# A long convolution and a mixture of experts in one kernel: hand-ordered joins between its outer and middle stages, and a middle that works on pairs of groups

## The chip, the cores and the metric

The kernel runs on one core of a Trainium2 chip. The metric is the device time of one execution in microseconds. Three executions were timed before the change; one more was recorded by the hardware profiler, and its trace is what the profile's rows come from.

## What is computed

The first half is a long convolution with a gate, the second a routed expert layer on its rows:

```python
def _attn_ref(x, v, pos_emb, w1, w2):            # x, v: (4, 11456, 128)
    h_filt = (np.maximum(pos_emb @ w1, 0.0) @ w2) * np.exp(-0.01 * pos)[:, None]
    Uf = np.fft.rfft(x * v, n=2 * S, axis=1)
    Hf = np.fft.rfft(h_filt, n=2 * S, axis=0)
    return x * np.fft.irfft(Uf * Hf[None], n=2 * S, axis=1)[:, :S, :]

def _moe_ref(x, modality_id, w_gate, modality_bias, w1, w2):   # x: (45824, 128), 8 experts
    logits = x @ w_gate + modality_bias[modality_id]
    e_idx = np.argmax(logits, axis=1)
    gate_w = softmax(logits)[np.arange(N), e_idx]
    for e in range(E):
        h = np.maximum(x[e_idx == e] @ w1[e], 0.0)             # 128 -> 1024
        out[e_idx == e] = gate_w[e_idx == e, None] * (h @ w2[e])
```

## The kernel before

**Stages.** A transform of length 90 x 64 stands in for the FFT. The filter is transformed first (`filter_stages`, `filter_middle`; its spectra go to `hs` in HBM). Then the four batches alternate between two kinds of stage. An *outer* stage b does three things in 16 steps q at once: the forward transform of batch b (`forward_stages`: load u and v, multiply, transform, copy to `A`), the inverse transform of batch b-1 (`inverse_stages`), and the routing of batch b-1's rows (`route_stages`), which works on 8 output blocks o of two q each. A *middle* stage (`middle_stages`) multiplies the spectra of batch b in 23 groups g of four of the 90 frequencies. Where an outer stage runs into the middle stage of its batch is called a join here; joins 1, 2 and 3 are those of batches 1, 2 and 3. After the last outer stage the expert tiles run (`experts`) to the end.

**A group of the middle stage.** `load(g)` asks on SyncE's queue for the constants b (256 KB) and the filter spectra h (512 KB), `load_c(g)` for the constants c (256 KB). `spectrum(g)` is 16 matmuls on TensorE (L598, 128 rows by 64 columns) into a pair of PSUM banks, pz, of which there are two. Then come its products on VectorE: two multiplications for `more` (L610), two for `part` (L617), one sum (L621). GpSimd does two sums of `more` (L612, L613) and one of `part` (L622). `inverse(g)` is 48 matmuls (L641, 64 rows by 128 columns) and two copies on ScalarE (L645). b, h and c lie in rings of three slots inside the tile `rings`; the outer stage keeps its transposed spectra `w_t` and the transposed rows `xT_t` in the same tile, so a slot can be asked for only when the outer stage no longer reads that place.

**What sets the order.** Every engine but GpSimd runs in the order in which the program calls it, and SyncE's queue of DMA requests too: a request that waits holds up all behind it. `steps` gives each stage function a step from a table (`OUTER`, `MID`: "name:delay"), `overlapped` lays the last steps of one stage beside the first of the next. In a join before the change the last three outer steps lie beside steps 1 to 3 of the middle stage. In a group's step the order is load_c, spectrum (with its products), the inverse of two groups back, load.

**Rows to their experts.** `store` writes an output block to `xr` (two DMAs of 366 KB), `places` writes the row numbers to `xi`. `fetch(b)` reads them back, `rows_back` brings 5 x 128 rows at a time into one of three buffers (18 requests per batch), and `send_rows` issues scatters of 128 rows from GpSimd (L270), 90 per batch, spread over the following middle and outer stage, at most 8 under way.

```python
MID = "load_c:2 spectrum:2 inverse:4 load:0"
OV, EA, EM = 3, 3, 5
```
```python
if b > 0:
    seq = seq[:-EM] + mid[:1] + seq[-EM:]
seq = overlapped(seq, mid[1:] if b else mid, OV if b else F3, b > 0)
```

## Time and profile before

| | us |
|---|---|
| median of three executions | 2121.38 |
| lowest, highest | 2119.81, 2122.85 |
| profiled execution, its own time | 2118.69 |
| its span, first to last instruction | 2116.9 |
| TensorE busy | 2049.2 |
| VectorE busy | 1709.5 |
| ScalarE busy | 1192.2 |
| GpSimd busy | 1195.1 |

The span is what the rows' times count in; the profiled execution took 1.8 us more than its span. A matmul's end is modelled, so the distance between two starts tells more than a duration. PE is TensorE, PEld its weight loads, DVE is VectorE, ACT ScalarE, POOL GpSimd, SPq SyncE's queue of DMA requests. A name after an arrow in brackets is what ended the idle time before a row.

### The profile page before, as it was taken

The page shows a single profiled execution, that of the slowest core. Times are in us where ns is not written, and L with a number is a line of the kernel's source. Part 1 is how long each engine was busy: PE and PEld are TensorE (multiplying, and loading weights), DVE is VectorE, ACT ScalarE, POOL GpSimd, SP SyncE. Part 2 cuts the span into 40 slices and gives each one's busy share as a digit, 9 for nine tenths or more (in the row PEclk, how much of TensorE's full clock was granted, in tenths as well). Part 3 has the DMA queues.
Part 4 walks back from the last instruction along what each step waited for, and adds up shares of the span by engine and source line. Part 5 has one row for each costly group of instructions (what it writes and reads, how often), then busy time and mean ns, then how long its engine had stood idle before and what let it go on. Part 6 is the DMA issues. An engine that isn't in the chain of part 4 may idle for free. (4 is left out here: it accounts for less than half of the span.)

```text
span 2116.9 us, 50221 instructions
## 1 busy us (share of the span) xinstructions
PE 2049.2 (97%) x18162; PEld 1668.1 (79%) x18162; DVE 1709.5 (81%) x2804; ACT 1192.2 (56%) x2166; POOL 1195.1 (56%) x1221
## 2 busy tenths in 40 slices
PE   8989999899999999899999999999999999999996
PEld 8888777687767877687668888888888888888896
DVE  2349767895779957896997888898898998888885
ACT  3642266324761267324666666666666666666674
POOL 0206500497547955497545677777777465555563
PEclk9999999999999999999999999999999999999998
DMA  9577677687879879885688466556565555555310
GB/s 314 214 294 235 234 231 244 217 265 262 302 257 291 263 259 325 271 265 191 207 245 280 83 132 127 124 122 133 125 129 116 111 109 95 100 97 97 79 42 26
DMA packets 509590, 397.55 MB, mean 188 GB/s; under 512 B 372697, under 2 KB 406317, under 8 KB 509337
## 3 DMA queue, kind: packets, MB, share of 16 engines
q1 hardware_dynamic: 482681, 334.90, 56.6%
q0 software_dynamic: 26496, 59.36, 7.9%
q8 instruction: 145, 2.38, 0.5%
q14 instruction: 108, 0.88, 0.1%
q10 hardware_dynamic: 160, 0.03, 0.0%
HBM read 290.58 MB, written 103.96 MB: 186 GB/s over the span
## 5 line engine op out<-in xcount | busy, mean ns | idle before, releaser
L1137 DVE SCALAR_TENSOR_TENSOR hl<-ph,hh 128x512 fp32r<-128x512 f32 x724 | 485.5, 678 | 105.2 <-ACT hh L1136 98.4
L1136 ACT ACTIVATE hh<-ph 128x512 fp32r<-128x512 f32 x724 | 425.2, 598 | 217.4 <-PE ph L1133 211.2
L270 POOL DMA_INDIRECT xs<-back,to x360 | 370.6, 1029 | 226.2 <-DVE y L677 72.6
L1186 POOL DMA_INDIRECT out<-ot,idx x362 | 400.2, 1106 | 144.1 <-issue 114.7
L1133 PE MATMUL ph<-xl,wh 128*128 128x512 f32 (+1 forms) x792 | 296.3, 374 | 4.5 <-DVE xl L1118 4.4
L1131 PE MATMUL ph<-xh,wh 128*128 128x512 f32 (+1 forms) x792 | 298.8, 377 | 0.7 <-ACT xh L1117 0.7
L1132 PE MATMUL ph<-xh,wl 128*128 128x512 f32 (+1 forms) x792 | 294.4, 372 | 1.1 <-DVE wl L1086 1.1
L1154 PE MATMUL po<-hh,wh 128*128 128x512 f32 (+1 forms) x792 | 294.3, 372 | 0.0
L1156 PE MATMUL po<-hl,wh 128*128 128x512 f32 (+1 forms) x792 | 293.8, 371 | 0.0
L1155 PE MATMUL po<-hh,wl 128*128 128x512 f32 (+1 forms) x792 | 293.7, 371 | 0.0
L645 ACT COPY A<-pw 128x512 f32<-128x512 f32 (+1 forms) x184 | 97.1, 579 | 345.1 <-PE pw L641 345.1
L617 DVE TENSOR_TENSOR part<-pz,rings 128x1024 f32<-128x1024 f32 (+1 forms) x184 | 211.3, 1189 | 2.2 <-POOL part L622 2.2
L612 POOL TENSOR_TENSOR more<-more 128x256 f32<-128x256 f32 (+1 forms) x92 | 76.8, 835 | 228.8 <-DVE more L610 217.4
L641 PEld LDWEIGHTS pw<-rings,part 64*128 64x128 f32 x2880 | 175.5, 188 | 35.4 <-issue 28.5
L641 PE MATMUL pw<-rings,part 64*128 64x128 f32 x2880 | 200.2, 278 | 2.5 <-POOL part L622 2.5
L598 PE MATMUL pz<-A,rings 128*64 128x256 f32 x1440 | 177.1, 388 | 13.7 <-DMA rings<-in_c_b 10.8
L466 PE MATMUL s<-fwd,seq 128*64 128x90 f32 x4096 | 170.7, 242 | 5.4 <-issue 4.0
L1133 PEld LDWEIGHTS ph<-xl,wh 128*128 128x128 f32 x792 | 149.3, 189 | 33.1 <-DVE xl L1118 5.8
L466 PEld LDWEIGHTS s<-fwd,seq 128*64 128x64 f32 x4096 | 161.3, 137 | 12.7 <-issue 4.7
L1132 PEld LDWEIGHTS ph<-xh,wl 128*128 128x128 f32 x792 | 149.6, 189 | 26.8 <-DVE wl L1086 1.6
L1131 PEld LDWEIGHTS ph<-xh,wh 128*128 128x128 f32 x792 | 149.4, 189 | 25.9 <-ACT xh L1117 0.9
L1154 PEld LDWEIGHTS po<-hh,wh 128*128 128x128 f32 x792 | 149.1, 188 | 26.1 <-issue 0.7
(190 smaller groups left out, 3662.4 us busy)
## 6 DMA issues: line engine op xcount, KB each, us to landing
rings<-hs SPq DMA_DIRECT2D x88, 512.0 KB
seq<-in_u SPq DMA_DIRECT2D x64, 512.0 KB
seq<-in_v SPq DMA_DIRECT2D x64, 512.0 KB
seq<-in_x SPq DMA_DIRECT2D x64, 512.0 KB
xr<-xo SPq DMA_DIRECT2D x64, 365.6 KB
back<-xr SPq DMA_DIRECT2D x72, 325.0 KB
rings<-in_c_b SPq DMA_DIRECT2D x88, 256.0 KB
rings<-in_c_c SPq DMA_DIRECT2D x88, 256.0 KB
```

The lines of the kernel that those rows point to most:

```text
L270: s = pool.indirect_dma_start(out=xs, out_offset=bass.IndirectOffsetOnAxis(ap=ix, axis=0), in_=src, in_offset=None, bounds_check=E * R - 1 ...
L466: pe.matmul(v[64 * c:64 * c + 64, blk, j], u[:, blk, 4 * h + j], fwd[:, c], start=True, stop=True)
L641: pe.matmul(pw[par][:, to:to + D], t[at], k["c"][at, q, c], start=i == 0, stop=i == len(terms) - 1)
L1131: pe.matmul(p, k[0, "h"][:, f:f + D], k["xh"], start=True, stop=False)
L1132: pe.matmul(p, k[0, "l"][:, f:f + D], k["xh"], start=False, stop=False)
L1133: pe.matmul(p, k[0, "h"][:, f:f + D], k["xl"], start=False, stop=True)
L1136: act.activation(hh, ph, AF.Relu)
L1137: dve.scalar_tensor_tensor(hl, ph, 0.0, hh.bitcast(F32), op0=ALU.max, op1=ALU.subtract)
L1154: pe.matmul(po, k[1, "h"][:, f], hh[:, t], start=g == 0, stop=False)
L1155: pe.matmul(po, k[1, "l"][:, f], hh[:, t], start=False, stop=False)
L1156: pe.matmul(po, k[1, "h"][:, f], hl[:, t], start=False, stop=g == NCH - 1)
L1186: s = pool.indirect_dma_start(out=out, out_offset=bass.IndirectOffsetOnAxis(ap=k["idx"][:, j:j + 1], axis=0), in_=ot[:, j, :], in_offset=N ...
```

## The change

It does six things. The joins of batches 1 to 3 are written out by hand, call by call, in `joined`: the routing of the last output block is taken out of the outer table and placed among the first groups, and the loads for groups 1 to 5 stand at chosen places, most of them ahead of the store of the last block. The ring places of h and b are changed, so that b of groups 1 and 2 no longer lies where `xT_t` lies and h of group 2 does. `spectrum` is split into the matmuls and `products`. From then on the middle stage works by twos: two spectra, their products, then two inverses of the pair before. In batches 1 to 3 the sum that VectorE did (L621) is GpSimd's for groups 0 to 4. The scatters of a middle stage run over groups 6 to 20 instead of 5 to 22, the others move into later stages, and all but the first of a batch's requests for rows are issued by ScalarE instead of SyncE. The second of the last inverse's two copies goes to VectorE, and there are 12 work buffers in place of 11.

```diff
-NA, NXO = 11, 3
+NA, NXO = 12, 3
...
-    def rows_back(b, k):
+    def rows_back(b, k, queue):
...
-        rows_back(b, 0)
+        rows_back(b, 0, sp)
...
-                rows_back(b, c // RC + 1)
+                rows_back(b, c // RC + 1, act)
...
-            ("h", 2 * GW, (8 * GW, 0, 2 * GW)),
-            ("b", GW, (10 * GW, 4 * GW, 5 * GW)),
+            ("h", 2 * GW, (8 * GW, 0, 4 * GW)),
+            ("b", GW, (10 * GW, 2 * GW, 3 * GW)),
...
-                if g == 4 and b > 0:
+                if g == (6 if b > 0 else -1):
                     fetch(b - 1)
...
-                dve.tensor_sub(p[:, 0], p[:, 0], part[1][:, 1])
+                (pool if b > 0 and g <= 4 else dve).tensor_sub(p[:, 0], p[:, 0], part[1][:, 1])
                 s = ins_of(pool.tensor_add(p[:, 1], p[:, 1], part[1][:, 0]))
-                if g > 4:
+                if 4 < g < NG - 2:
                     send_rows(1 + (g % 3 == 0), s)
...
-                    act.copy(A[:, k0:k0 + 2 * n - 1:2].rearrange("p k b n -> p k (b n)"),
+                    copy = dve.tensor_copy if par and g == NG - 1 else act.copy
+                    copy(A[:, k0:k0 + 2 * n - 1:2].rearrange("p k b n -> p k (b n)"),
...
-            todo = dict(inverse=inverse, spectrum=spectrum, load_c=load_c, load=load)
-            return [(int(t), todo[n]) for n, t in (w.split(":") for w in MID.split())]
+            two = lambda g: g - g % 2
+            table = [(lambda g: two(g) + 2, spectrum), (lambda g: two(g) + 2, products),
+                     (lambda g: min(two(g) + 5, NG + 3), inverse), (0, load), (2, load_c)]
+            by_hand = 6 if b > 0 else 0
+            return steps(NG, table)[by_hand:], dict(
...
-                      1 + (b == nb - 1 and q % 3 > 0))
+                      1 + (b == nb - 1))
...
+            return (seq[:-3] + do("load0") + seq[-3:-2] + do("load1", "load_c0", "load_b2") + seq[-2:-1]
+                    + do("spectrum0") + seq[-1:]
+                    + do("half", "products0", "spectrum1", "logits", "load_h2", "load3",
+                         "products1", "spectrum2", "lturn", "load_c1", "products2",
+                         "inverse0", "load4", "load_c2", "spectrum3", "shift", "biased", "choice",
+                         "inverse1", "load5", "load_c3", "store", "products3")
+                    + mid[:1] + do("send") + keep + mid[1:2] + do("places") + mid[2:])
...
-            if lo == 0 and 3 * at % 10 < 3:
+            if lo == 0 and at % 3 == 0:
                 send_rows(1)
```

In `joined`, "half", "logits", "lturn", "shift", "biased", "choice", "send", "store" and "places" are the routing of the last output block (o = 7): transposes of its rows, matmuls with the gate, a transpose of the logits, the bias, its addition, the choice of an expert, the row numbers, the writes to `xr` and `xi`.

**TensorE in a join.** pr are the matmuls of row numbers, xT and lt transposes, pl the logits, pz a spectrum, pw an inverse. Before, from the row numbers of block 6 to the spectrum of group 2 (the first row of pz is groups 0 and 1):

```order
L797 MATMUL pr<-sc_101,both 128x8
L710 MATMUL xT<-ident,xo_90 128x109 x8
L724 MATMUL pl<-rings,wg 32x436 x4
L734 MATMUL lt<-ident,lT 109x128 x4
L598 MATMUL pz<-A,rings 64x256 x16
L792 LDWEIGHTS both
L792 MATMUL pr<-oh_100,both 128x128
L794 LDWEIGHTS both
L794 MATMUL pr<-sc_102,both 128x128
L797 LDWEIGHTS both
L797 MATMUL pr<-sc_102,both 128x8
L598 MATMUL pz<-A,rings 64x256 x8
```

Now:

```order
L813 MATMUL pr<-sc_101,both 128x8
L603 MATMUL pz<-A,rings 64x256 x8
L726 MATMUL xT<-ident,xo_90 128x109 x8
L603 MATMUL pz<-A,rings 64x256 x8
L740 MATMUL pl<-rings,wg 32x436 x4
L603 MATMUL pz<-A,rings 64x256 x8
L750 MATMUL lt<-ident,lT 109x128 x4
L651 MATMUL pw<-rings,part 128x128 x8
```

The last block's transposes, logits and their transpose now stand between the spectra of groups 0, 1 and 2 and the inverse of group 0; its row numbers, which stood ahead of the spectrum of group 2, come after that of group 5.

**SyncE's queue in a join.** xr<-xo is a store of an output block, the buffer's number telling which (xo_90 block 5, xo_88 block 6, xo_89 block 7), in_c_b, hs and in_c_c are b, h and c of a group. Before:

```order
L579 DMA rings<-in_c_b 128x512
L582 DMA rings<-hs 128x1024
L783 DMA xr_58<-xo_90 90x1x1040 x2
L783 DMA xr_58<-xo_88 90x1x1040 x2
L579 DMA rings<-in_c_b 128x512
L582 DMA rings<-hs 128x1024
L587 DMA rings<-in_c_c 128x512
L579 DMA rings<-in_c_b 128x512
```

Now:

```order
L799 DMA xr_58<-xo_90 90x1x1040 x2
L578 DMA rings<-in_c_b 128x512
L583 DMA rings<-hs 128x1024
L799 DMA xr_58<-xo_88 90x1x1040 x2
L578 DMA rings<-in_c_b 128x512
L583 DMA rings<-hs 128x1024
L592 DMA rings<-in_c_c 128x512
L578 DMA rings<-in_c_b 128x512
```

Group 0's loads now stand behind the store of block 5; the loads of group 1 and all after them stand behind the store of block 6 in both. The store of block 7 stood ahead of c of group 2 and now stands ahead of b of group 6.

**TensorE in the steady middle**, a few groups on. Before:

```order
L598 MATMUL pz<-A,rings 64x256 x8
L641 MATMUL pw<-rings,part 128x128 x8
L641 MATMUL pw<-rings,more 128x128 x4
L641 MATMUL pw<-rings,part 128x128 x8
L641 MATMUL pw<-rings,more 128x128 x4
L598 MATMUL pz<-A,rings 64x256 x8
```

Now:

```order
L603 MATMUL pz<-A,rings 64x256 x16
L651 MATMUL pw<-rings,part 128x128 x8
L651 MATMUL pw<-rings,more 128x128 x4
L651 MATMUL pw<-rings,part 128x128 x8
L651 MATMUL pw<-rings,more 128x128 x4
L651 MATMUL pw<-rings,part 128x128 x8
L651 MATMUL pw<-rings,more 128x128 x4
L651 MATMUL pw<-rings,part 128x128 x8
L651 MATMUL pw<-rings,more 128x128 x4
L603 MATMUL pz<-A,rings 64x256 x16
```

Two spectra and two inverses now follow each other where one of each did.

## Rows read from the trace of the kernel before

**Rows 1.** Timeline of PE, batch 0's middle stage: start us, us, engine, instructions, [idle before].
```profile
149.69 3.67 PE L598 MATMUL pz<-A,rings 128*64 128x256 f32 x32 [0.85 <-ACT A L469]
155.34 1.95 PE L598 MATMUL pz<-A,rings 128*64 128x256 f32 x16 [1.97 <-issue]
...
164.85 1.52 PE L598 MATMUL pz<-A,rings 128*64 128x256 f32 x12
...
254.25 1.06 PE L641 MATMUL pw<-rings,part 64*128 64x128 f32 x16
...
256.93 1.06 PE L641 MATMUL pw<-rings,part 64*128 64x128 f32 x16
...
259.17 2.01 PE L664 MATMUL wt<-ident,A 128*90 128x128 f32 x16 [0.73 <-ACT A L645]
```

**Rows 2.** Timeline of PE: S6 of batches 1, 2; last inverses of 1 to 3.
```profile
416.16 1.95 PE L598 MATMUL pz<-A,rings 128*64 128x256 f32 x16
...
500.17 0.94 PE L641 MATMUL pw<-rings,part 64*128 64x128 f32 x12 [1.04 <-POOL part L622]
...
659.79 1.52 PE L598 MATMUL pz<-A,rings 128*64 128x256 f32 x12
...
743.21 0.94 PE L641 MATMUL pw<-rings,part 64*128 64x128 f32 x12 [0.46 <-POOL part L622]
...
985.43 0.94 PE L641 MATMUL pw<-rings,part 64*128 64x128 f32 x12 [0.97 <-POOL part L622]
```

**Rows 3.** Timeline of PE in joins 1 and 2.
```profile
393.44 3.54 PE L598 MATMUL pz<-A,rings 128*64 128x256 f32 x16 [3.14 <-DMA rings<-in_c_b]
...
628.83 0.94 PE L710 MATMUL xT<-ident,xo 109*128 109x109 f32 x8
...
636.46 1.95 PE L598 MATMUL pz<-A,rings 128*64 128x256 f32 x16 [1.87 <-DMA rings<-in_c_b]
```

**Rows 4.** Timeline of SyncE's queue, b of group 1 in joins 1 and 2.
```profile
386.89 1.61 SPq L579 DMA_DIRECT2D rings<-in_c_b  x1
...
631.17 1.61 SPq L579 DMA_DIRECT2D rings<-in_c_b  x1
```

**Rows 5.** Windows: busy us of PE, PEld, DVE, ACT, POOL; PEclk, DMA share, GB/s.
```profile
394.00:396.00 2.00, 2.00 (x12) 1.10 (x10) 1.75 (x2) 0.00 (x0) 1.23 (x2) 0.50 0.99 365
...
502.50:505.90 3.40, 3.40 (x18) 2.84 (x19) 0.00 (x0) 1.79 (x4) 1.04 (x2) 0.50 0.89 319
```

**Rows 6.** Timeline of DVE in join 1: choice of block 7, products of group 1.
```profile
388.46 0.29 DVE L750 TENSOR_TENSOR lg<-lt,lg 109x128 f32<-109x128 f32 x1 [1.70 <-PE lt L734]
...
391.51 0.12 DVE L776 TENSOR_SCALAR xo<-small 109x16 f32<-109x16 f32 x1
...
397.03 1.29 DVE L610 TENSOR_TENSOR more<-pz,rings 128x512 f32<-128x512 f32 x2 [1.24 <-PE pz L598]
398.24 2.34 DVE L617 TENSOR_TENSOR part<-pz,rings 128x1024 f32<-128x1024 f32 x2
```

**Rows 7.** Timeline of DVE and POOL: the sums of `part`, batches 1 and 2.
```profile
423.25 2.10 DVE L621 TENSOR_TENSOR part<-part 128x512 f32<-128x512 f32 x1
423.48 1.31 POOL L622 TENSOR_TENSOR part<-part 128x512 f32<-128x512 f32 x1
...
428.85 0.69 DVE L621 TENSOR_TENSOR part<-part 128x512 f32<-128x512 f32 x1
...
666.46 1.75 POOL L622 TENSOR_TENSOR part<-part 128x512 f32<-128x512 f32 x1
...
672.54 1.26 POOL L622 TENSOR_TENSOR part<-part 128x512 f32<-128x512 f32 x1
...
676.82 1.26 POOL L622 TENSOR_TENSOR part<-part 128x512 f32<-128x512 f32 x1
```

**Rows 8.** Groups by line, DVE, 660 to 730 us: busy us, mean ns, idle before.
```profile
L621 DVE TENSOR_TENSOR part<-part 128x512 f32<-128x512 f32 x15 | 14.9, 994 | 0.5
```

**Rows 9.** Waits of SyncE's queue, 265 to 1000 us: us in total, times, longest.
```profile
SPq L254 <- DMA xs<-back,to: 122.1, 36, 7.4
```

More of the change, by code (lines that the diff above doesn't have):

```diff
@@ L63 @@
 FIRST = "forward:17 load:0 product:16"
-MID = "load_c:2 spectrum:2 inverse:4 load:0"
 OV, EA, EM = 3, 3, 5
@@ L248, in after_all @@
             tc.add_manual_dep(ins_of(x), q.name, sync_dep, reason="every scatter")
-    def rows_back(b, k):
+    def rows_back(b, k, queue):
         if k < NB:
             of = xr[b].rearrange("(p k c) r -> p k c r", p=D, c=RC)
-            sp.dma_start(back_t[(b * NB + k) % 3], of[:, k])
+            queue.dma_start(back_t[(b * NB + k) % 3], of[:, k])
     def fetch(b):
         sp.dma_start(to_t[b % 2], xi[b].rearrange("(p c) -> p c", p=D))
-        rows_back(b, 0)
+        rows_back(b, 0, sp)
         waiting.extend((b, c) for c in range(NR // D))
@@ L575, in middle_stages, with load_b, load_h, load @@
             kept = {}
-            def load(g):
+            def load_b(g):
                 k = kept[g] = {"b": of_group(g, ring("b", g)).rearrange("p (j d) -> p j d", d=D)}
                 sp.dma_start(k["b"], of_group(g, a["c_b"][g]).rearrange("p (j d) -> p j d", d=D))
+            def load_h(g):
                 t, n = ring("h", g), 2 * D * len(k1s(g))
-                k["h"] = spectra(g, t)
+                kept[g]["h"] = spectra(g, t)
                 sp.dma_start(t[:, 0:n], hs[g][:, 0:n])
+            def load(g):
+                load_b(g)
+                load_h(g)
             def load_c(g):
@@ L601, in spectrum, with products @@
                                       start=True, stop=True)
-                z = pz[:, 0:n].rearrange("p q (c b d) -> p q c b d", c=2, b=2)
-                h = k["h"]
+                k["z"] = pz[:, 0:n].rearrange("p q (c b d) -> p q c b d", c=2, b=2)
+            def products(g):
+                k = kept[g]
+                n = len(k1s(g)) // 2
+                z, h = k.pop("z"), k["h"]
                 part = [new_a("part")[:, 0:n * 4 * D].rearrange("p (c q b d) -> p c q b d", c=2, b=2, d=D)
@@ L644, in inverse @@
                     k0 = G * g + par
-                    act.copy(A[:, k0:k0 + 2 * n - 1:2].rearrange("p k b n -> p k (b n)"),
+                    copy = dve.tensor_copy if par and g == NG - 1 else act.copy
+                    copy(A[:, k0:k0 + 2 * n - 1:2].rearrange("p k b n -> p k (b n)"),
                              pw[par][:, 0:2 * D * n].rearrange("p (q x) -> p q x", q=n))
-            todo = dict(inverse=inverse, spectrum=spectrum, load_c=load_c, load=load)
-            return [(int(t), todo[n]) for n, t in (w.split(":") for w in MID.split())]
+            two = lambda g: g - g % 2
[3 more added lines that the diff above has]
+            return steps(NG, table)[by_hand:], dict(
+                load=load, load_b=load_b, load_h=load_h, load_c=load_c,
+                spectrum=spectrum, products=products, inverse=inverse)
         def inverse_stages(b):
@@ L852, in outer_steps @@
             if 0 < b < nb:
-                later.append([lambda f=todo[n]: f(NQ - 1) for n in ("store", "places")])
-                todo["store"] = but_last(todo["store"], 2)
+                for name in ("half", "logits", "lturn", "shift", "biased", "choice", "send", "store", "places"):
+                    later[b, name] = lambda f=todo[name]: f(NQ - 1)
+                    todo[name] = but_last(todo[name], 1)
                 todo.pop("places")
@@ L862, in early, with joined @@
             return first[:at] + [second[0]] + first[at:] + second[1:]
-        later = []
+        def joined(b, seq):
+            mid, of = middles[b]
+            do = lambda *names: [(lambda f=of[n[:-1]], g=int(n[-1]): f(g)) if n[-1].isdigit() else later[b, n]
+                                 for n in names]
+            bases = {nb - 2: base1, nb - 1: base2}
+            keep = [lambda: dve.tensor_copy(bases[b], base)] if b in bases else []
+            return (seq[:-3] + do("load0") + seq[-3:-2] + do("load1", "load_c0", "load_b2") + seq[-2:-1]
[5 more added lines that the diff above has]
+                    + mid[:1] + do("send") + keep + mid[1:2] + do("places") + mid[2:])
+        later = {}
+        middles = [middle_stages(b) for b in range(nb)]
         seq = overlapped(steps(NQ, filter_stages()), steps(NG, filter_middle()), F1)
@@ L870, in hyena_moe_kernel @@
                 extra = [lambda b=b: bias_load(b - 1)] + [lambda: None] * 2 + [bias_flag]
-                at = len(seq) - 24
+                at = len(seq) - 20
                 for k, g in enumerate(extra):
@@ L874, in hyena_moe_kernel @@
             seq = early(seq, outer_steps(b), EA) if b else overlapped(seq, outer_steps(b), F2)
-            if b == nb - 2:
-                seq[-1] = lambda f=seq[-1]: (f(), dve.tensor_copy(base1, base))
-            if b == nb - 1:
-                seq[-1] = lambda f=seq[-1]: (f(), dve.tensor_copy(base2, base))
-            if b < nb:
-                mid = steps(NG, middle_stages(b))
-                for k, g in enumerate(later.pop() if b else ()):
-                    mid[3 + k] = lambda f=mid[3 + k], g=g: (f(), g())
-                if b > 0:
-                    seq = seq[:-EM] + mid[:1] + seq[-EM:]
-                seq = overlapped(seq, mid[1:] if b else mid, OV if b else F3, b > 0)
+            if 0 < b < nb:
+                seq = joined(b, seq)
+            elif b == 0:
+                seq = overlapped(seq, middles[b][0], F3)
         scratch = []
@@ L947, in rest @@
     def rest():
+        assert not waiting and len(scatters) == nb * NR // D, (len(waiting), len(scatters))
         sp.dma_start(pad, a["c_pad"].rearrange("p (j r) -> p j r", j=TH // D))
```

## The prediction, made before the change was run

> **What bounds the kernel now.** I read the page's busy lines first: TensorE is busy for nearly the whole span, so a change pays only where it shortens the chain of matmuls or removes one of the short waits in it. The change touches the first half of the program alone, the four middle stages and the three joins before them, so next I read TensorE's timeline there.
>
> In the steady middle nothing waits, yet one group takes (164.85 - 155.34) / 2 = 4.755 us [rows 1]. Its parts take less. Two spectra in a row last 3.67 us and one lasts 1.95, so a spectrum adds 1.72; one inverse follows another after 256.93 - 254.25 = 2.68 [rows 1]. That makes 4.40. The other **0.36 us per group is the price of going from a spectrum to an inverse and back**, where the shape of the matmuls changes.
>
> At a join the chain does wait. S0, S1, ... stand for the spectra of groups 0, 1, ..., P0 and I0 for their products and inverses. At the end of a middle stage the last inverse waits 1.04, 0.46 and 0.97 us for GpSimd's last sum [rows 2], and the first transpose after it 0.73 us for ScalarE's last copy [rows 1]. At the start S1 waits 3.14 and 1.87 us in the first two joins for its constants b1 [rows 3]. SyncE asks for b1 at 386.89 and 631.17 [rows 4], right behind the store of output block 6, which waits for that block's choice. So b1 arrives 6.5 and 5.3 us after it is asked for.
>
> **Switches.** Before, 21 runs of inverses stand between spectra in a middle stage; now pairs stand together. In batch 0 there are 11 runs, so 10 x 0.36 = 3.6 us go. In batches 1 to 3 the runs from S6 on fall from 17 to 9, so 8 x 0.36 = 2.9 each, 8.6 in all (what lies before S6 belongs to the join). **Sum -12.2.** This needs VectorE to keep up. P takes 398.24 + 2.34 - 397.03 = 3.55 us without its last sum [rows 6], with it some 4.2, so 8.4 per pair beside TensorE's 2 x 4.40 + 0.36 = 9.16.
>
> **Start of batch 0.** S3 now stands ahead of I0, and there are two pz buffers, so S3 waits for P1. S2 already waits 1.97 us for P0 [rows 1]; P1 comes one P, 4.2 us, later, at about 159.5. S3, I0, I1 (1.8, 2.7, 2.7) follow and S4 starts at 166.8 in place of 164.85: **+2.0.**
>
> **Joins**, with the times of the second. The choice of block 6, its store and b1's place behind that store are unchanged, so S1 can't start before 636.46 [rows 3]. The small matmuls of block 6 end as the eight transposes start, at 628.83 [rows 3]. Now S0 (1.95) comes first and then those transposes (0.94), which reach 631.7, and TensorE has nothing for 4.7 us. What followed such a pause: in the first join S1, after 3.14 us without work, took 3.54 us in place of 1.95 [rows 3], and the granted clock was 0.50 of full speed, the 1.2 GHz level, over all of 394 to 396 [rows 5]. I charge 1.3 of those 1.6 us in joins 2 and 3, and all of it in join 1, so S1 ends at 639.7. From there VectorE's order decides: P1, P2, the choice of block 7, P3, and S5 needs P3's buffer. P is 3.55 (these groups' last sum is GpSimd's now). The choice is some 0.8 of shifts and 391.63 - 388.46 = 3.2 [rows 6], so 4.0. Before, it lay in TensorE's wait ahead of S1; now it stands on the path. P2's spectra h2 can be asked for only after the logits that stand behind S1; I charge 0.5 for that. So S5 starts at 639.7 + 3 x 3.55 + 4.0 + 0.5 + 0.1 = 655.0, and with S5, the place matmuls, I2 and I3 (1.8 + 0.3 + 5.5) S6 starts at 662.6. Before it started at 659.79 [rows 2]: **+2.8 in join 2**, and I take the same for join 3. In join 1 S1 ends at 393.44 + 3.54 = 396.98 as before, so S6 starts at 396.98 + 22.9 = 419.9 in place of 416.16 [rows 2]: +3.7. **Sum +9.3.** The low bound has no fall of the clock, no wait for h2, and in join 1 b1 after 5.3 us: +1.0, +1.0 and +0.4, 2.4 in all. The high bound is a second stretch at the lower level, 1.6 us more each: 14.
>
> The five sums moved to GpSimd cost it some 1.3 us each (1.26 [rows 7]) where it has no scatters, so nothing on the path, and take 0.6 us off each P above, which the 3.55 already holds. The multiplications of P, with one operand in PSUM, kept their 2.34 while GpSimd worked on the same group [rows 6]; a VectorE sum with both operands in SBUF took 2.10 in place of 0.69 while GpSimd's sum ran [rows 7]. No such sum of VectorE's is left in these groups. The Trainium skill's Perfetto Trace Analysis (Optimizing Scalar/DVE Operations) warns that the two share an SBUF read port, so that moving operations between them "might not help". By that rule each join would be 1.8 us longer and the sum below +1.2; the trace agrees with it for sums from SBUF only, and I keep the 3.55.
>
> **GpSimd after S6.** A group with one scatter takes it 676.82 - 672.54 = 4.28 us, one with two 672.54 - 666.46 = 6.08 less the 0.49 by which the first sum there was stretched, so 5.6 [rows 7]. Groups 6 to 20 are now 5 with two and 10 with one: 70.8 us, and groups 21 and 22 some 4.9. TensorE needs 15 x 4.58 = 68.7 for the same fifteen. GpSimd starts about 3.2 us after S6, and the first scatter waits some 1.5 for its rows, so I22 could start at S6 + 80.4; TensorE alone would reach it at S6 + 80.0. I charge **+0.7 each, +2.1**; bounds 0 and 2 each.
>
> **Ends.** The waits of I22 go, as groups 21 and 22 have no scatters: **-2.5**. The last copy of each middle stage is split over ScalarE and VectorE; of the 0.73 us about 0.3 goes: **-1.2** for four. After the first of these pauses the clock stood at 0.50 from 502.5 to 505.9 [rows 5]; with a shorter pause it stays up: **-1.7**, bounds -1.7 and 0.
>
> **SyncE to ScalarE.** Of 18 requests for rows per batch 17 move to ScalarE's queue. ScalarE idles in the middle and has slack elsewhere: 0; gone wrong, it is a rival below. One scatter more per three steps in the last outer stage and a few more among the expert tiles: 0, GpSimd waits there.
>
> **The sum:** -12.2 + 2.0 + 9.3 + 2.1 - 2.5 - 1.2 - 1.7 = **-4.2 us**, from 2118.69 to 2114.5 for the profiled execution. That lies 2.7 under the median of the three runs shown, 2121.38, so 2117.2; I say **2117.0**. No change means within 0.2%, about what a measurement of this kernel can tell: 2117.1 to 2125.6. The forecast stands on that border.
>
> **Rivals.**
> *Cheap joins.* The clock holds, h2 is in time and GpSimd keeps up: the joins cost 2.4 and GpSimd nothing: 2121.4 - 4.2 - 6.9 - 2.1 = 2108. For it: in join 2 S1 kept its 1.95 us after a wait of 1.87 [rows 3]. Against: the empty stretch is now longer than any of those.
> *Joins closed.* b1 is there when S0 ends. Then S1 ends at 633.7 instead of 639.7, a gain of 6 to 7.6 per join: 2117 - 20 = 2097. Against: the order of SyncE's queue, in which b1 still stands behind the store of block 6.
> *GpSimd and VectorE block each other, slower.* Place: groups 6 to 20 of batches 1 to 3. VectorE has 9.16 / 2 - 4.2 = 0.4 us per group to spare, and its sum took 0.99 on average in batch 2 [rows 8], 0.3 over the 0.69, where TensorE took 4.755. If closer packing makes that 0.7, a group takes 4.9: 45 x 0.3 = 13.5 more, 2131. It decides from 0.4 on. For it: single waits of 1.4 [rows 7]. Against: the mean stretch of 0.3 is a fifth of that.
> *ScalarE held up, slower.* The requests for rows waited 122.1 us in all, 36 times, for scatters [rows 9], mean 3.4. If a quarter of these waits falls on ScalarE and a third of it reaches TensorE, 10 us: 2127. Against: SyncE asks ahead, and ScalarE gets to the same place several us later. The Trainium skill's DMA: Bandwidth & Descriptors (Anatomy of one DMA, SWDGE path) puts such a wait on the issuing sequencer, before dispatch; that speaks for this rival, as copies behind the request would wait too.
>
> **Chances.** Forecast 0.52, whose own range is 2112 to 2123; cheap joins 0.22; joins closed 0.05; blocking 0.13; ScalarE 0.08. Of the forecast's share I put 0.19 below the border and 0.33 above it. Faster by over 0.2%: 0.19 + 0.22 + 0.05 = 0.46. Within 0.2%: 0.33 + 0.03 from mild blocking = 0.36. Slower by over 0.2%: 0.18. The range 2107 to 2127 takes in cheap joins and the mild cases of the two slower ones, and leaves out some 0.15.
>
> **What would show it.** Right: spectra in pairs with no gap between, TensorE at 9.16 us per pair, S1 still waiting for b1 in each join, now 4 to 6 us, S5 waiting for P3, no wait ahead of I22. Wrong: S1 right behind S0 (the gain is then much larger); over 9.3 us per pair in groups 6 to 20 with waits on GpSimd's or VectorE's sums; ScalarE standing at a request for rows.

## The result, and the profile after the change

The changed kernel takes 2131.57 us (median of 5 runs, 2131.43 to 2135.51) beside 2121.38 us for the kernel before in the same session (5 runs, 2118.68 to 2122.85): a ratio of 1.0051, 95% interval 1.0039 to 1.0062. It is slower, by more than twice the 0.2% named in the prediction, and above the range of 2107 to 2127. The profiled execution took 2131.82 us with a span of 2130.0, 13.1 us over the 2116.9 of before.

Below, a **join** is the time from the first place matmul of block 6 (`pr`) to the start of S6, and the **rest** the time from S6 to the end of I22. First the windows of the changed kernel that hold join and rest of batches 1, 2, 3; the columns are the window, its length, busy us (and instructions) of PE, PEld, DVE, ACT, POOL, then PEclk, DMA share and GB/s.

```profile
385.34:425.35 40.01, 30.61 (x315) 21.83 (x315) 29.53 (x50) 5.23 (x13) 22.66 (x23) 0.87 0.69 216
425.35:507.04 81.69, 81.55 (x1153) 68.50 (x1152) 72.46 (x85) 20.82 (x40) 70.83 (x71) 1.00 0.80 263
632.50:671.50 39.00, 29.99 (x314) 21.47 (x314) 30.21 (x51) 5.33 (x13) 23.18 (x24) 0.87 0.69 222
671.50:753.17 81.67, 81.56 (x1153) 68.51 (x1152) 72.12 (x85) 20.83 (x40) 71.24 (x72) 1.00 0.80 260
878.76:917.81 39.05, 29.70 (x314) 21.32 (x314) 30.25 (x51) 5.33 (x13) 23.20 (x24) 0.87 0.69 222
917.81:999.32 81.51, 81.51 (x1153) 68.52 (x1152) 73.60 (x85) 20.83 (x40) 71.10 (x72) 1.00 0.77 253
```

The same stretches of the kernel before:

```profile
384.00:416.16 32.16, 28.18 (x314) 20.04 (x314) 28.59 (x52) 5.78 (x14) 15.24 (x15) 0.95 0.86 276
416.16:501.55 85.39, 84.35 (x1154) 68.39 (x1152) 78.47 (x91) 20.40 (x38) 77.82 (x79) 1.00 0.80 260
628.29:659.79 31.50, 26.73 (x314) 19.79 (x314) 29.17 (x54) 5.78 (x14) 15.80 (x15) 1.00 0.87 280
659.79:744.60 84.81, 84.35 (x1154) 68.39 (x1152) 78.52 (x90) 20.40 (x38) 78.65 (x78) 1.00 0.79 255
870.17:901.50 31.33, 26.66 (x315) 19.59 (x315) 29.02 (x53) 5.77 (x14) 15.68 (x15) 1.00 0.85 278
901.50:986.82 85.32, 84.34 (x1154) 68.38 (x1152) 76.25 (x89) 20.40 (x38) 78.45 (x79) 1.00 0.77 246
```

The rest now has TensorE busy throughout (81.55 of 81.69), where it had some 84.35 us of work and up to 1 us of waits. The join has it idle for 9 us, at a mean clock of 0.87. The 13.1 us are made up so:

| part | before | after | us |
|---|---|---|---|
| up to S0 of batch 0 | 149.69 | 150.38 | +0.7 |
| batch 0, S0 to the end of I22 | 108.75 | 109.49 | +0.7 |
| three joins | 94.99 | 118.06 | +23.1 |
| three rests | 255.52 | 244.87 | -10.6 |
| end of each I22 to the next `pr` | 377.87 | 376.52 | -1.4 |
| what follows the last middle stage | 1130.1 | 1130.7 | +0.6 |

Now TensorE's timeline, in the changed kernel as in all that follows with the columns of [rows 1 to 3]: a pair of the steady middle in batch 0, the end of batch 1's middle stage, and batch 0's start.

```profile
178.59 3.67 PE L603 MATMUL pz<-A,rings 128*64 128x256 f32 x32
...
187.75 3.67 PE L603 MATMUL pz<-A,rings 128*64 128x256 f32 x32
```

```profile
502.97 0.94 PE L651 MATMUL pw<-rings,part 64*128 64x128 f32 x12
...
507.68 1.98 PE L680 MATMUL wt<-ident,A 128*90 128x128 f32 x16 [0.64 <-DVE A L656]
```

```profile
156.02 2.64 PE L603 MATMUL pz<-A,rings 128*64 128x256 f32 x16 [1.97 <-issue]
160.21 3.68 PE L603 MATMUL pz<-A,rings 128*64 128x256 f32 x16 [1.54 <-issue]
...
169.43 2.81 PE L603 MATMUL pz<-A,rings 128*64 128x256 f32 x24
```

A pair takes 187.75 - 178.59 = 9.16 us, as forecast, and no wait is shown ahead of I22 any more, where [rows 2] have 1.04, 0.46 and 0.97. The first transpose still waits 0.64 us where [rows 1] have 0.73. In batch 0 S3 waits 1.54 us; S2 in part and S3 wholly run at the lower clock (2.64 and 3.68 us in place of 1.95; the mean granted clock from 156 to 164 is 0.57). S4 starts at 169.43.

Join 1 on TensorE:

```profile
385.96 1.95 PE L603 MATMUL pz<-A,rings 128*64 128x256 f32 x16
387.84 0.97 PE L726 MATMUL xT<-ident,xo 109*128 109x109 f32 x8
393.58 3.68 PE L603 MATMUL pz<-A,rings 128*64 128x256 f32 x16 [4.78 <-DMA rings<-in_c_b]
397.19 1.68 PE L740 MATMUL pl<-rings,wg 128*32 128x436 f32 x8
398.81 2.26 PE L603 MATMUL pz<-A,rings 128*64 128x256 f32 x16
...
409.67 1.95 PE L603 MATMUL pz<-A,rings 128*64 128x256 f32 x16
415.20 2.41 PE L603 MATMUL pz<-A,rings 128*64 128x256 f32 x16 [3.58 <-issue]
...
417.88 2.08 PE L651 MATMUL pw<-rings,part 64*128 64x128 f32 x16
...
422.47 1.04 PE L651 MATMUL pw<-rings,part 64*128 64x128 f32 x13 [0.45 <-ACT A L656]
```

The rows are S0, the transposes of block 7, S1, the logits, S2, S4, S5, and parts of I2 and I3. S1 waits 4.78 us for b1 ([rows 3] had 3.14) and then takes 3.68 us. S5 waits 3.58 us, and it and I2 run slowly again. S1 itself starts hardly later than before the change: from `pr` to S1 the three joins take 8.24, 8.20 and 8.32 us, and took 9.44, 8.17 and 7.97. What the joins lose, they lose from S1 on. VectorE says what S5 waits for (line, operation, and in brackets the idle time before):

```profile
397.30 1.29 DVE L620 TENSOR_TENSOR more<-pz,rings 128x512 f32<-128x512 f32 x2 [5.80 <-PE pz L603]
...
402.99 1.29 DVE L620 TENSOR_TENSOR more<-pz,rings 128x512 f32<-128x512 f32 x2 [2.14 <-DMA rings<-hs]
...
406.46 0.28 DVE L757 TENSOR_TENSOR lg<-wf,bias 109x128 f32<-109x128 f32 x1
406.97 1.25 DVE L759 TENSOR_TENSOR lg<-lg,score 109x128 f32<-109x128 f32 x1
...
411.57 1.27 DVE L620 TENSOR_TENSOR more<-pz,rings 128x512 f32<-128x512 f32 x2
...
415.02 1.28 DVE L620 TENSOR_TENSOR more<-pz,rings 128x512 f32<-128x512 f32 x2
```

P1 starts when S1 ends; P2 waits 2.14 us for h2; the choice of block 7 takes 406.46 to 411.57; P3 follows and ends as P4 starts, at 415.02, and S5 starts at 415.20. SyncE's queue shows why b1 and h2 are late:

```profile
386.38 1.78 SPq L799 DMA_DIRECT2D xr<-xo  x2
388.27 1.60 SPq L578 DMA_DIRECT2D rings<-in_c_b  x1
...
398.95 0.33 SPq L583 DMA_DIRECT2D rings<-hs  x1
```

The store of block 6 is asked for at 386.38, b1 behind it at 388.27, and h2 only at 398.95, after the logits. Counted from `pr`, b1 is asked for as before the change (2.93 us; 2.89 from [rows 4]).

### The profile page after: what moved, and what is told of

The parts are those of the page before. It is cut to its first block, busy times and chain, and to the rows that moved or that the text cites. A ratio compares the mean times of both kernels' runs of the same rounds, so it can differ in the third digit from the quotient of the medians.

```text
span 2130.0 us, 50283 instructions
## 1 busy us (share of the span) xinstructions
PE 2046.4 (96%) x18162; PEld 1672.9 (79%) x18162; DVE 1700.6 (80%) x2793; ACT 1190.2 (56%) x2162; POOL 1201.2 (56%) x1236
## 5 line engine op out<-in xcount | busy, mean ns | idle before, releaser
L656 ACT COPY A<-pw 128x512 f32<-128x512 f32 x180 | 96.0, 584 | 322.3 <-PE pw L651 322.3
L603 PEld LDWEIGHTS pz<-A,rings 128*64 128x64 f32 x1440 | 103.9, 142 | 86.1 <-issue 37.9
```

## The experiments

Each kernel was compared with the kernel before on the same chip, with 5 to 12 executions of it; the kernel before had medians of 2120.8 to 2121.4 us in these sessions. The joins and rests come from each kernel's own trace, read as above; batch 0 is S0 to the end of I22.

| kernel | us (median) | ratio to before, 95% | joins | rests | batch 0 |
|---|---|---|---|---|---|
| before | 2121.4 | 1 | 32.2, 31.5, 31.3 | 85.4, 84.8, 85.3 | 108.8 |
| after | 2131.6 | 1.0039 to 1.0062 | 40.0, 39.0, 39.1 | 81.7, 81.7, 81.5 | 109.5 |
| e2 store of 6 behind b1 | 2115.1 | 0.9953 to 0.9978 | 34.0, 32.7, 34.7 | 81.7, 81.7, 81.5 | 109.3 |
| e3 choice ahead | 2119.7 | 0.9986 to 1.0003 | 32.4, 33.9, 32.0 | 83.8, 83.6, 85.5 | 109.3 |
| e4 pause filled | 2125.3 | 1.0003 to 1.0025 | 36.1, 36.3, 35.5 | 83.0, 85.3, 84.1 | 109.5 |
| e5 pairs alone, on before | 2116.1 | 0.9964 to 0.9983 | 32.1, 30.9, 31.4 | 85.5, 84.8, 83.8 | 107.6 |
| e6 = e2 + e3 | 2114.6 | 0.9961 to 0.9981 | 30.3, 30.3, 30.3 | 85.2, 86.7, 86.0 | 108.0 |
| e7 sums on VectorE | 2138.4 | 1.0067 to 1.0093 | 40.1, 40.8, 38.8 | 83.0, 83.1, 85.4 | 109.6 |
| e8 rows on SyncE | 2131.0 | 1.0031 to 1.0057 | 38.9, 38.6, 38.8 | 83.3, 81.5, 83.1 | 109.3 |
| e9 one by one | 2133.2 | 1.0048 to 1.0074 | 34.3, 34.5, 34.4 | 88.7, 85.5, 87.9 | 108.8 |
| e10 batch 0 single | 2127.7 | 1.0025 to 1.0051 | 38.7, 38.5, 38.6 | 81.7, 81.7, 82.8 | 106.1 |
| e11 = e6 + e10 + places later | 2112.3 | 0.9938 to 0.9964 | 31.5, 31.5, 31.5 | 82.1, 81.7, 86.7 | 107.6 |
| e12 = e11 + scatters | 2105.6 | 0.9911 to 0.9937 | 31.5, 30.3, 30.3 | 83.8, 82.7, 84.0 | 107.8 |
| e13 six single | 2127.0 | 1.0017 to 1.0040 | 34.5, 34.4, 34.2 | 85.7, 83.7, 88.0 | 106.4 |
| e14 = e12 + six single | 2107.7 | 0.9924 to 0.9950 | 29.8, 31.0, 29.7 | 82.5, 83.2, 84.1 | 106.4 |

The theory: the joins lose, by b1's place behind a store, by two falls of the clock, and by VectorE's order; the pairs gain. The rivals: ScalarE's requests, GpSimd's sums, or pairs that don't gain.

### e2: the store of block 6 behind b1

```diff
+                later[b, "store6 "] = lambda: store(NO - 2)
+                todo["store"] = but_last(todo["store"], 3)
...
-  do("load1", "load_c0", "load_b2")
+  do("load1", "load_c0", "load_b2", "store6 ")
```

> The changed kernel, with one thing moved in each join: the store of block 6 is asked for after the constants b1, h1, c0 and b2, and no longer ahead of them. Theory (S1 waits 4.8 us because b1 lies behind that store on its way, and the clock falls in that pause): S1's wait goes to about 2 us or less, the first half-clock stretch of 6.83 us goes with it, and each join is 4 to 7 us shorter, so the median is 2112 to 2120. Rival (b1 is late by its own bytes, or by the requests of b0 and h0 ahead of it, not by the store): S1 waits over 4 us as before and the time stays within 2 us of 2131.6.

S1 (first row) no longer waits; S5 (second) still does:

```profile
388.52 1.95 PE L603 MATMUL pz<-A,rings 128*64 128x256 f32 x16
...
407.72 3.68 PE L603 MATMUL pz<-A,rings 128*64 128x256 f32 x16 [3.80 <-issue]
```

The joins are 6.0, 6.3 and 4.4 us shorter, and the time falls by 16.4 us. So b1's place in the queue is what S1 waits for; its own bytes are not. No other single edit of the changed kernel takes as much off the time. But b1 stood behind that store before the change, too: the exchange takes away an old wait, and with it the joins' time comes near the old one. The half clock has moved behind S5's wait.

### e3: the choice of block 7 ahead of S1

```diff
-  "half", "products0", "spectrum1", "logits", "load_h2", "load3", "products1", "spectrum2", "lturn",
-  "load_c1", "products2", "inverse0", "load4", "load_c2", "spectrum3", "shift", "biased", "choice"
+  "half", "products0", "logits", "shift", "lturn", "biased", "choice", "spectrum1", "load_h2", "load3",
+  "products1", "spectrum2", "load_c1", "products2", "inverse0", "load4", "load_c2", "spectrum3"
```

> The changed kernel, with the choice of block 7 moved forward: its logits, their turn, shift, biased and choice stand ahead of S1 and the products of group 1, in the time in which TensorE waits for b1, so that h2, which takes the place of block 7's turned rows, can also be asked for earlier. Theory (what holds S5 is VectorE: products 1, a wait of 2.1 us for h2, products 2, choice of 5.2 us, products 3): the waits before S5 (3.0 to 3.6 us) and the second half-clock stretch (3.41 us) go, S1's wait of 4.8 us stays, and each join is 3 to 6 us shorter: 2114 to 2122. Rival (S5 is held by ScalarE's copies or by GpSimd's sums, and VectorE has room): the waits before S5 stay and the time stays within 2 us of 2131.6.

S1, then S4 and S5 in one row, then a spectrum of the next pairs:

```profile
392.67 3.63 PE L603 MATMUL pz<-A,rings 128*64 128x256 f32 x16 [1.99 <-DMA rings<-in_c_b]
...
406.39 3.67 PE L603 MATMUL pz<-A,rings 128*64 128x256 f32 x32
...
429.12 1.95 PE L603 MATMUL pz<-A,rings 128*64 128x256 f32 x16 [1.29 <-DMA rings<-in_c_b]
```

S5 follows S4 with no gap, and the joins are 7.6, 5.1 and 7.0 us shorter: 19.7 of the 23.1 us that they had lost, with b1 where it was. So most of that loss came from the routing of block 7 behind S1, with the late h2 and S5's wait that follow from it. S1's wait shrank to 1.99 only because the logits and their turn now fill part of it: b1 is as late as before, 8.39 us after `pr` (392.67 - 384.28) beside 8.24. What was not expected is the last row: with a shorter join the constants of a later group come late, and the rests give back 2.1, 1.9 and 4.0 us.

### e4: TensorE kept at work in the pause

```diff
-  do("half", "products0", "spectrum1", ...
+  do("half", "products0") + [warm] + do("spectrum1", ...
```

`warm` is 40 transposes of a constant into a bank that nobody reads.

> The changed kernel, with 40 transposes of a constant on TensorE between the products of group 0 and S1 in each join (some 4.7 us of work at the full clock by the 0.94 us of the 8 transposes of block 7, and nobody reads what they write). They add work, in the pause only. Theory (the clock falls because TensorE pauses for 4.8 us ahead of S1, and that fall costs 3.4 us per join): the half-clock stretch of 6.83 us that begins with S1 is gone, S1 starts at the same time or up to 0.5 us later, and the time is 6 to 11 us lower, 2121 to 2126. Rival (the fall belongs to something else, or the time it costs is hidden under VectorE's chain up to S5): 2130 to 2134.

The filler, and S1 behind it:

```profile
390.42 4.53 PE L884 MATMUL warm<-ident 128*128 128x128 f32 x40
396.06 1.95 PE L603 MATMUL pz<-A,rings 128*64 128x256 f32 x16 [1.11 <-DMA rings<-in_c_b]
```

S1 starts 0.7 us later after `pr` here (at the same place to 0.1 us in the other joins) and takes 1.95 us in place of 3.68. The joins are 3.9, 2.7 and 3.6 us shorter though TensorE has more to do. In joins 1 and 3 no half clock is left, so there the two falls cost some 3.9 and 3.6 us; join 2 keeps one (PEclk 0.50 from 653.9 to 657.2), behind a wait of I1 for VectorE. The time drops by 6.3 us; the rests give 1.3, 3.6 and 2.6 back here too (the profiled run is 5 us above the median of this kernel).

### e5: pairs from S6 on, on the kernel before

```diff
-  (spectrum, with its products: group g at step g+2), (inverse: g+4)
+  (spectrum, products: step g+2 up to g=5, then g - g%2 + 2), (inverse: g+4 up to g=3, then g - g%2 + 5)
+  (c of g=6 and later: asked for after the inverses of its step)
```

A first build, e1, lacked the last line. It asked for c7, c9, ... ahead of the inverse that still reads their place, so that these inverses used another group's constants and waited 121.9 us in all for them. Its 2294.6 us say nothing on the theory.

> The kernel before with its joins untouched: only the middle stage goes by twos from the spectrum of group 6 on in every batch (one by one before that, in batch 0 too), with one buffer more for the products. Theory (the pairs gain, the joins lose): from the start of S6 to the end of I22 each of batches 1 to 3 takes 81.5 to 82.5 us in place of 85.2 (a pair 9.16 us), and batch 0 gains about as much, so the median is 13 us lower than before: 2108, between 2105 and 2112. Rival 1 (the pairs gain only because the change also puts products on GpSimd and requests on ScalarE, or VectorE holds the pair up without that): 2115 to 2121. Rival 2 (the pairs cost something elsewhere, in the ends of the middle stages): 2121 or above.

> The kernel before with its joins untouched: only the middle stage goes by twos from the spectrum of group 6 on in every batch (one by one before that, in batch 0 too), with one buffer more for the products. In the first build of this idea the constants c of a group were asked for ahead of the inverse that still read the place; here c6 and later ones are asked for after it. Theory (the pairs gain, the joins lose): from the start of S6 to the end of I22 each of batches 1 to 3 takes 81.5 to 82.5 us in place of 85.2 (a pair 9.16 us), and batch 0 gains about as much, so the median is some 13 us lower than before: 2108, between 2105 and 2112. Rival 1 (the pairs gain only because the change also puts sums on GpSimd and requests on ScalarE, or constants come late for pairs without its order of requests, as after e3 and e4, where S6 to I22 took 82.9 to 85.5 us): 2113 to 2121. Rival 2 (the pairs cost something elsewhere, in the ends of the middle stages): 2121 or above.

The time is 2116.1, in the first rival's range: the pairs give 1.2 us in batch 0 and nothing, nothing and 1.6 in the rests. The theory that the pairs shorten the kernel by themselves falls. They do shorten TensorE's own work, from 84.35 to 82.1, 81.8 and 82.0 us in the rests, but waits take it back: with the old joins the pairs wait at their start (S7 for 1.04, 1.05 and 0.50 us), and I22 now waits 2.00, 1.90 and 1.07 us for GpSimd's last sum, where the scatters still run up to group 22.

### e6: both edits

> The changed kernel with the edits of e2 and e3 together: the store of block 6 after b1, h1, c0 and b2, and the choice of block 7 ahead of S1. Theory: the two waits are separate, and each edit takes away the one that the other leaves (S5's wait of 3.8 us after e2, S1's of 2.0 us after e3), so the joins go to 29.5 to 31 us, with little or no half clock in them; then either the middle keeps its 81.7 us (2101 to 2107), or the constants now come too late for the pairs, as they did after e3 (83.7 us), and half of it is given back: 2107 to 2112. Rival (both edits work on one wait, so they don't add): 2113 to 2117, as e2 alone.

The time, 2114.6, lies in the rival's range, 0.5 us from e2's, but the joins decide against the rival: all three take 30.3 us with no half clock in them, better than before the change. So the edits do work on two waits, though not by their sum (16.7 and 19.7 us apart, 27.0 together). The rests give it back: 85.2, 86.7, 86.0. So "then the constants come too late" it is, and worse than I allowed. TensorE's late spectrum, SyncE's queue ahead of it, and a window of the pause:

```profile
426.26 3.06 PE L603 MATMUL pz<-A,rings 128*64 128x256 f32 x16 [2.03 <-DMA rings<-in_c_b]
```

```profile
409.64 0.33 SPq L592 DMA_DIRECT2D rings<-in_c_c  x1
414.04 0.80 SPq L826 DMA_DIRECT2D xi<-ix  x2
...
417.85 0.34 SPq L257 DMA_DIRECT2D to<-xi  x1
...
418.71 0.42 SPq L578 DMA_DIRECT2D rings<-in_c_b  x1
```

```profile
416.00:420.00 4.00, 4.00 (x66) 3.54 (x64) 3.97 (x6) 0.30 (x1) 2.61 (x3) 1.00 0.37 87
```

From 410 to 414 SyncE stands at the store of block 7's row numbers (`xi<-ix`), which waits for VectorE; then it stands at the fetch that reads them back (`to<-xi`) until 417.85. No constants are asked for meanwhile, and the DMA engines drop to 87 GB/s. What it asks for from 418.71 on lands too late.

### e7 and e8: the two rivals named in the prediction

```diff
-  (pool if b > 0 and g <= 4 else dve).tensor_sub(p[:, 0], p[:, 0], part[1][:, 1])
+  dve.tensor_sub(p[:, 0], p[:, 0], part[1][:, 1])
```

> The changed kernel with the subtraction of groups 0 to 4 back on VectorE in batches 1 to 3 (five times 0.69 us more for VectorE in each join, five sums of 1.3 us less for GpSimd). Theory (VectorE's chain holds S5, the first four sums lie in it, or beside the wait for h2): the waits before S5 grow by 0.5 to 2.5 us, and the time by 1.5 to 7 us: 2133 to 2138. Rival (GpSimd's sums hold the products, or slow VectorE while they run, and were the mistake): 2125 to 2130.

```diff
-  rows_back(b, c // RC + 1, act)
+  rows_back(b, c // RC + 1, sp)
```

> The changed kernel with the requests of rows for the scatter back on SyncE's queue. Theory (ScalarE loses nothing by them): within 2 us of 2131.6, the joins within 0.5 us each; SyncE's own wait of 7.4 us for a free place may come back and make it up to 2 us slower. Rival (ScalarE's copies behind the requests stand in the way, in the middle or in the joins): 2122 to 2128.

With the five sums back on VectorE the kernel is 6.8 us slower: moving them was right. But it does not pay where the theory had it. S5's waits change by -0.1, +1.0 and +0.5 us and the joins by +0.1, +1.8 and -0.3; the rests are 1.3, 1.5 and 3.9 us longer (see the table of pauses below). With the rows back on SyncE it is the same: 1.0031 to 1.0057 beside 1.0039 to 1.0062. Neither rival caused the loss.

### e9, e13: what the pairs are worth, and where

```diff
-  (spectrum, products: step g - g%2 + 2), (inverse: g - g%2 + 5)
+  e9:  (spectrum, products: g+2), (inverse: g+4) for all groups
+  e13: the same for spectra 0 to 5 and inverses 0 to 3, pairs behind them
```

> The changed kernel with its joins and everything else, but the middle stages one group at a time (spectrum, products, inverse) in place of two at a time. Theory (a spectrum between two inverses costs 0.36 us of switching, so the pairs save 8 or 9 times that in each middle stage, in a kernel whose joins leave VectorE and the constants time to get ahead): S6 to the end of I22 takes 84.5 to 85.5 us in place of 81.6, batch 0 takes 1 to 4 us more or, as it starts one by one, no more, and the time is 2139 to 2147. Rival (the pairs gain nothing of their own, the 81.6 us come from the late start, after which VectorE and the constants are ahead): within 3 us of 2131.6.

> The changed kernel with the first six groups one by one in every batch and pairs from S6 on. Theory (spectra 4 and 5 side by side are what makes S5 wait in the join, since both need a pair of banks that VectorE frees late; with the inverse of group 2 between them the wait is covered): from pr to S6 34 to 35 us as in e9, in place of 39 to 40, and S6 to I22 between 81.7 and 84 us, so the time is 2112 to 2122. Rival (VectorE is behind by then in either order, and what the join saves the middle gives back): from pr to the end of I22 120 to 122 us as after the change and in e9, and the time 2127 to 2131.

One by one, the rests are 3.8 to 7.0 us longer (1.2 to 3.7 of it are waits for constants; TensorE's own work is 2.7 us more in batches 2 and 3, near the 8 x 0.36 = 2.9 of the prediction), the joins 4.6 to 5.7 shorter, and the time is the same (1.0048 to 1.0074 beside 1.0039 to 1.0062). So inside the join the pair of S4 and S5 costs what the pairs gain later: with I2 between them S5's wait for P3 is covered. e13 takes the better half of each, and the joins are indeed 34.2 to 34.5; but the rests rise to 85.7, 83.7 and 88.0, and 4.6 us are won, of which batch 0 has 3.1. The rival held: what the join saves is given back. SyncE in e13, at the fetch of the row numbers:

```profile
418.67 0.36 SPq L708 DMA_DIRECT2D md<-in_moe_modality_id  x1
423.60 0.34 SPq L257 DMA_DIRECT2D to<-xi  x1
```

SyncE asks for nothing for nearly 5 us, the same place as in e6. VectorE, which the rival named, has a part in it: S7 and S8 wait 0.86 and 0.81 us for its products in batch 1, and S9 then 2.19 us for its constants.

### e10: batch 0 starts one by one

```diff
-  pairs from S0 on in batch 0
+  spectra 0 to 5 and inverses 0 to 3 of batch 0 one by one
```

> The changed kernel, with the first six groups of batch 0 taken one by one as before, pairs from S6 on. Theory (S3 of batch 0 waits 1.5 us for a pair of banks that VectorE still reads, and the clock falls there): S0 to the end of I22 of batch 0 is 107 to 108 us in place of 109.5, and the time is 1 to 3 us lower, 2128.5 to 2130.5. Rival (that stretch is bound by VectorE's products in either order): within 0.5 us of 109.5, and no change.

S0 to the end of I22 takes 106.1 us in place of 109.5, and the time is 3.9 us lower: the pair at the very start was a loss, as forecast, and a larger one.

### e11, e12, e14: the row numbers later

```diff
-  mid[:1] + do("send") + keep + mid[1:2] + do("places") + mid[2:]
+  mid[:1] + do("send") + keep + mid[1:4] + do("places") + mid[4:]
-  if g == (6 if b > 0 else -1): fetch(b - 1)
+  if g == (8 if b > 0 else -1): fetch(b - 1)
   # e12, besides e11:
-  send_rows(1 + (g % 3 == 0), s)
+  send_rows(1 + (g % 2 == 0), s)
   # e14: e12 with the edit of e13
```

> The changed kernel with e2's, e3's and e10's edits together, and the store of block 7's row numbers and the fetch that reads them two groups later (after I4 and I5, and with the products of group 8). After e6 SyncE stood from 410 to 418 us at these two and asked for the constants of groups 8 to 10 late, so that S9 waited 2.0 us and the clock fell. Theory (that wait on SyncE is what took back the gain of e6's joins): the joins stay at 30 to 31 us, S6 to the end of I22 goes from 86 to 82 to 83.5 us, and the time is 2099 to 2106. Rival (in a closed join the constants come late by their bytes, or VectorE is behind, whatever SyncE does): S6 to I22 stays at 85 to 86 us and the time is 2111 to 2115.

The rests of batches 1 and 2 come down to 82.1 and 81.7, in joins of 31.5: the gain of e6's joins stays. SyncE still stands at the fetch (in batch 1 from 421.68 to 425.86), but it no longer stands at the store as well. Batch 3's rest is 86.7, and the time, 2112.3, is in the rival's range. There SyncE stands at the next request, of rows:

```profile
902.68 0.35 SPq L257 DMA_DIRECT2D to<-xi  x1
907.72 0.34 SPq L253 DMA_DIRECT2D back<-xr  x1
```

> e11's kernel, with the number of scatters that each middle stage issues brought back to 20: e11 began two groups later and issued 17, so that by batch 3 SyncE stood 5 us at the fetch of rows (from 903 to 907.7 us) for a buffer that scatters still read. Theory (that wait alone made batch 3's S6 to I22 86.7 us, beside 81.7 to 82.1 us in batches 1 and 2): batch 3 goes to 82 to 83 us and the time is 2105 to 2109. Rival (the last batch is late for another reason): no change, 2110 to 2113.

> e12's kernel with the first six groups one by one in every batch. Theory of e13: S5 has no wait left in e11's joins, since the choice is done early, so two switches of 0.36 us come back and the time is within 3 us of e12's. Rival (VectorE is behind at S4 and S5 here too, only hidden): 3 to 8 us faster than e12.

With 20 scatters per middle stage in place of 17 that wait is gone (the same two requests stand at 907.62 and 908.26), and batch 3's rest is 84.0, not quite the 82 to 83 forecast. The row numbers keep SyncE from asking for b, h or c of any group for a while in each batch. That pause goes along with the rests:

| kernel | pause in the three batches, us | rests, us |
|---|---|---|
| after | 5.3, 4.7, 6.6 | 81.7, 81.7, 81.5 |
| e2 | 5.1, 4.7, 6.7 | 81.7, 81.7, 81.5 |
| e3 | 7.7, 7.9, 8.6 | 83.8, 83.6, 85.5 |
| e6 | 8.7, 8.8, 9.3 | 85.2, 86.7, 86.0 |
| e7 | 7.7, 7.3, 8.2 | 83.0, 83.1, 85.4 |
| e11 | 6.0, 4.7, 9.2 | 82.1, 81.7, 86.7 |
| e13 | 7.2, 6.4, 9.6 | 85.7, 83.7, 88.0 |

In all the kernels above with the new joins a pause of 6.7 us or less stands beside rests of 81.5 to 84.1, one of 7.0 or more beside 82.8 to 88.7. That the two go together is no proof of a cause; e11's edit is the test of it, and its batch 3, where the pause stayed long, agrees. In e12 the pauses are 6.0, 4.9 and 6.4, but the rests have another wait, that of I22 for GpSimd's last sum, which the change had taken away (1.02, 1.07 and 1.00 us):

```profile
496.96 0.94 PE L651 MATMUL pw<-rings,part 64*128 64x128 f32 x12 [1.02 <-POOL part L632]
```

The median of e12, 2105.6, is in the theory's range, and 15.4 us faster than the kernel before, 26 faster than the changed one: the best here, with an interval of 0.9911 to 0.9937. The profiled execution took 2112.7, and in it joins and rests together are only 2.4 us shorter than in e11's; where its other executions gained more, no trace shows. e14 is within 3 us of it, as the theory said: once the choice is early, S4 and S5 may stand together.

## Why the prediction was wrong

**Switches, -12.2.** The price was right: 9.16 us per pair, and TensorE's own work in a rest fell by 2.8 us (84.35 to 81.55) where 2.9 was forecast. Rests and ends together were forecast at -8.6 + 2.1 - 2.5 = -9.0 and measured -10.6. But the term is no gain of its own: whether the time falls with TensorE's work hangs on the waits around it. On the kernel before it gave 4.7 us in all (e5); in the changed kernel the same order costs as much in the join as it gives behind it (e9).

**GpSimd after S6, +2.1.** Did not occur: the rests took 81.5 to 81.7, TensorE's own 81.6. VectorE's sums averaged 0.83 us in batch 2's rest, 0.94 in the same stretch before, so the blocking rival had nothing under it either.

**Joins, +9.3. This is the step that failed: measured +23.1.** The mechanism was right in every link: S1 waits for b1 behind block 6's store (forecast 4.7 us, measured 4.78, 4.73 and 4.86), the clock falls, then P1, h2, P2, choice, P3 hold S5. The sizes were not: +2.8 was forecast for joins 2 and 3 and +3.7 for join 1, and +7.9 for join 1, +7.5 and +7.7 for the others were measured. For join 1 I had S6 35.9 us after `pr`; it came after 40.01. S1 ended 1.1 us earlier than forecast. From its end to S5 I had 15.25 us and the trace has 17.9: h2 2.14 in place of 0.5, the choice 5.1 in place of 4.0. From S5 to S6 I had 7.6 and the trace has 10.15: a second fall of the clock, of which I had priced one at the high bound of 14 only, and 0.45 for a copy. The high bound of 14 took in the second fall alone, not the longer h2 and choice with it. By e3 the routing of block 7 behind S1, with what follows from it, is the larger part (19.7 of the 23.1 us); by e4 the two falls of the clock are 3.6 to 3.9 us of a join.

Of the choice's 1.1 us, 0.96 is one instruction: L759 took 1.25 us, beside 0.29 as the median of its 31, while a sum moved to GpSimd ran there (from 406.77, for 1.30 us); joins 2 and 3 show the same (1.24). The move is not to blame: in e7, with the moved sums back on VectorE, the choice takes 5.1 us as well, and there it is L757 that is slow (0.28 us in the changed kernel), beside the sum that GpSimd had all along:

```profile
405.79 1.36 DVE L757 TENSOR_TENSOR lg<-wf,bias 109x128 f32<-109x128 f32 x1
```

That is the rule I had weighed, in the Trainium skill's Perfetto Trace Analysis (Optimizing Scalar/DVE Operations), that the two share a read port: the trace agrees, but on an operation that I had not looked at. By e7 the move of the sums is nonetheless worth 6.8 us.

**Start of batch 0, +2.0.** With its part of the switches I had -1.6; measured +0.7. S3 waited as forecast, but the clock fell there too, and I had priced no fall. Single, it is 3.4 us shorter (e10).

**Ends and the split copies, -2.5 and -1.2.** I22's waits went as forecast. The transposes still wait 0.64 us: the split gave under 0.1 each, not 0.3.

**Clock at 502.5, -1.7.** Right: the granted clock is 1.00 from 502.0 to 508.5, and the stretch from I22 to `pr` is 1.3 us shorter there.

**SyncE to ScalarE, 0.** Right (e8). The page that I had set beside this rival, the Trainium skill's DMA: Bandwidth & Descriptors (Anatomy of one DMA, SWDGE path), puts the wait on the issuing sequencer; the trace agrees in one place only, where a copy of ScalarE came 1.0 us late by scatters, and by e8 it costs nothing.

Of the 17.3 us between forecast and measured span, 13.8 lie in the joins, 2.3 in batch 0, 1.5 between I22 and `pr` and 1.3 in what the sum had at nothing (ahead of S0 and behind the last middle stage); the rests gave 1.6 back.

What stays open: e6 and e13 show SyncE's stand and the late constants together, and e11 that moving the requests gives the rests of two batches back; no run asks for the row numbers on another queue. Of the rest's 82.7 to 84.0 us in e12, TensorE's waits are 1.1 to 2.0, and 1.0 of that is GpSimd's last sum each time.

## What to carry to other kernels

Price a wait that you lengthen with everything that comes after it: what the clock does to the next microseconds, and who is then next in line; two links that are each hidden now are both on the path once they stand in a row. An order that saves time per step may only pay where the supply is ahead: before counting the gain, look for the request queue's next head-of-line wait (here the round trip of the row numbers on SyncE) and move it. And where a request stands behind a store on one queue, try the exchange of the two first: it was a small edit, and worth 16 us.

## What the runs showed of the hardware that was not expected

The pause of 4.8 us ahead of S1 was followed by the 1.2 GHz level in every join of the changed kernel, and so was the one of 3.0 to 3.6 us ahead of S5 (PEclk, third from the end, in two windows of join 1):

```profile
393.60:399.40 5.80, 5.80 (x28) 2.47 (x30) 2.10 (x3) 0.43 (x1) 1.32 (x2) 0.50 0.37 139
416.60:419.90 3.30, 3.30 (x27) 2.44 (x25) 3.30 (x5) 0.00 (x0) 3.30 (x4) 0.50 0.89 257
```

Filler work in the pause took it away (e4: S1 1.95 us in place of 3.68). But the same pause cost different amounts. In e10, whose joins have the same order, S1 took 3.39 us after the same wait, and the logits and S2 behind it ran at the full clock again (0.94 and 1.95 us, in place of 1.68 and 2.26); that join took 38.7 us in place of 40.0:

```profile
388.82 3.39 PE L603 MATMUL pz<-A,rings 128*64 128x256 f32 x16 [4.77 <-DMA rings<-in_c_b]
```

Where such stretches fall may be why executions of one kernel differ. The mean granted clock goes along with the time in those that spread most, 0.996 at 2104.1 us and 0.992 at 2112.7 in e12, 0.996 at 2118.9 and 0.992 at 2130.5 in e4; that it is the cause was not tested.
